# Loading the last two batches of an attention and Fourier-mixing kernel in natural token order

## The chip, the cores and the metric

The kernel runs on one core of a Trainium2 chip. A core has five engines, each with its own in-order stream of instructions: TensorE (PE in the profile; its weight loads are shown apart as PEld), VectorE (DVE), ScalarE (ACT), GpSimd (POOL) and SyncE (SP), which here only issues DMAs. DMAs are issued from the queues of SP, ACT and POOL, and all of them are carried out by the same 16 DMA engines. The metric is the device time in microseconds of one execution, the median of several runs.

## The reference

Four batches, 8 heads, 768 tokens, 64 numbers per head. First comes attention in which a token sees the first 8 keys (global) and the last 96 (local), with a bias that falls with distance; then, on the 768x512 result `x` of each batch, the real part of a two-dimensional Fourier transform, a normalization and a two-layer network with a ReLU:

```python
rel = pos[:, None] - pos[None, :]
is_global = pos[None, :] < 8
is_local = (rel >= 0) & (rel < 96)
dist = np.where(is_global & ~is_local, 96.0, np.abs(rel))
scores = scale * q @ k.T - slopes * dist          # -1e9 where neither holds
a = softmax(scores);  x = a @ v                   # heads side by side: (4, 768, 512)
X = np.fft.fft(np.fft.fft(x, axis=1), axis=2)
u = x + np.real(X)
un = (u - mean(u)) / np.sqrt(var(u) + 1e-6)
out = u + np.maximum(un @ w_ch1, 0.0) @ w_ch2     # 512 -> 2048 -> 512
```

## The kernel before

**Stages.** Each batch `b` goes through four stages. *Attention* works on pairs of heads (`hp` 0 to 3, numbered through as `n = 4*b + hp`): q and k are loaded and cast to fp16 (`load_qk`), transposed (`trans`), multiplied into three groups of scores (`score`, tile `sc`), passed through an exponential on ACT and multiplied by v (`av`, tile `pav`). The 8 global keys have their own small product (`glob`, tile `pgl`), for which the first 32 transposed keys were copied together into `kG` (`kg_copies`, line 494). *Mixing* folds the 768 tokens by their symmetries on VectorE (`fold_s`, `fold_d`), multiplies by a table of sines and cosines along the tokens (`y_unit`, line 933, tiles `py` and `zy`) and by a second one along the features (`u_unit`, line 1023, tile `pu`). Part of the results is also needed with its columns reversed: `mirror` (lines 968 to 970, tile `rev`) copies it on POOL. From batch 1 on the attention result also goes out to DRAM and back in another order (`bounce`, lines 735 to 745, `xd` and `xr`). *Normalization* (`centre`, lines 1108 to 1125, with a square root on POOL in the small tile `sm`) follows. The *network* runs in units `c = 3*b + pair`: eight `ph` units of 8 matmuls against the first weights (line 1178) and then `pg` units against the second (line 1211; from c = 8 on in a form with seven products for eight, `pgA` and `pgD`, line 1295). The sum of output and `u` (line 1220) is stored by SP (line 1225) or, for one pair of each batch, by an indirect DMA from POOL (line 1195).

**Token order.** Within each block of 128 tokens all four batches are kept with the even tokens in partitions 0 to 63 and the odd ones in partitions 64 to 127 (`tau` in the code). Batches 0 and 1 get this order from the way in which pairs of rows of 512 bytes are loaded and transposed on TensorE. Batches 2 and 3 (`b >= FB`) are loaded by half: for each pair of heads and each of q and k four loads (two halves of the partitions, two heads, line 433), and for v two loads (line 419), each taking every second row of 256 bytes. With eight loads for q and k and two for v that is 4 x 10 = 40 loads per batch, all issued from POOL's queue. Their transposes are DMA transposes on SP's queue (line 505). The masks, the distance matrix `dist_k` (copied on POOL at line 1447 from a tile `dist` that batches 0 and 1 use) and the transform's table `t1` follow the same order.

**The order of the work.** A planner in the kernel's own program (`Plan`) holds a modelled time for each engine, and takes at each step what can start first: a TensorE unit out of four streams (mixing, attention, `ph`, `pg`) or a waiting operation of another engine. Each operation has a price in us written beside it; `pl.later([("POOL", 1.0, fn)], needs, ...)` says engine, price, and what must be there. Where two engines are named, the one that ends sooner by the model gets it. A table `BIAS` shifts the start of single operations or groups of them, and so changes the order. Prices and table set only the order of the instructions in each engine's stream; on the chip each engine goes strictly through its own stream and waits on semaphores. A software DMA on POOL (`swq`) may have eight of its kind in flight in the model.

**Buffers.** q and k of n >= 6 rotate through 4 buffers, the transposed ones (`TT`) through 4, so batch 3's transposes wait for batch 2's scores and global products. The loads of batches 2 and 3 wait for the last weight load (`("wl", 7)`), those of v also for the end of the attention two batches before. There is one buffer for the mixing tiles `zy`, one for `rev`.

Of the kernel before, what the change touches and what calls it, by code (L numbers as in the profile page):

```python
# [14 lines left out]
P = 128  # L15
# [7 lines left out]
class Plan:  # L23
# [125 lines left out]
    def slot(self, tag):  # L149
# [7 lines left out]
    BIAS = {('h', 7, 2): 1.5, ('g0', '*', 1): 1.5, ('ss', '*', 7): 1.5, ('rd', '*', 10): -0.3, ('u', 3, 0): 1.5, (1, 19): 0.3,  # L157
# [88 lines left out]
def kernel(  # L246
# [23 lines left out]
    FB = 2  # L270
    DB = 0
# [12 lines left out]
    X3 = [(1, 1), (1, 2), (2, 1), (2, 2), (3, 1)]  # L284
# [7 lines left out]
    t1 = np.zeros((P, 4, 384))  # L292
    for r in range(4):
        th = 2.0 * np.pi * ((tau[:, None] * (6 * mm + r)) % S) / S
        t1[:, r, 0:128] = np.sin(th)
        t1[:, r, 128:256] = np.cos(th)
        t1[:, r, 256:384] = -np.sin(th)
    t1x = np.zeros((P, 5, 384))
    for n, (r, i) in enumerate(X3):
        th = 2.0 * np.pi * (((tau[:, None] + P * i) * (6 * mm + r)) % S) / S  # L300
        t1x[:, n, 0:128] = np.sin(th)
        t1x[:, n, 128:256] = np.cos(th)
        t1x[:, n, 256:384] = -np.sin(th)
# [21 lines left out]
    t1_d = nc.inline_tensor(t1.reshape(P, -1).astype(np.float16), name="t1m")  # L325
    t1x_d = nc.inline_tensor(t1x.reshape(P, -1).astype(np.float16), name="t1xm")
# [49 lines left out]
    t1_sb = kon.tile([P, 4, 384], FP16, tag="t1", name="t1")  # L376
# [38 lines left out]
    def load_v(b, hp):  # L415
        h0 = 2 * hp
        for t in range(2):
            def run(t=t):
                nc.gpsimd.dma_start(v16[b % 2][64 * t:64 * t + 64, h0:h0 + 2, :, 0:Dh].rearrange("m h i d -> m (h i) d"),  # L419
                                    v[b, h0:h0 + 2].rearrange("h (i m t) d -> t m (h i) d", m=64, t=2)[t])  # L420
            swq(run, 0.75, ([("avdone", b - 2), ("wl", 7)] if b > 1 else []), [("v", b, hp, t)], 0.7, b < 2)

    def load_qk(b, hp):
# [3 lines left out]
        for w, src in enumerate((q, k)):  # L427
            if b >= FB:
                for x in range(4):
                    def run(w=w, src=src, t=x // 2, h=x % 2):  # L430
                        if n not in qk16:
                            qk16[n] = buf(tag, ti, [P, 2, NS, 2, Dh], FP16, 1)
                        nc.gpsimd.dma_start(qk16[n][64 * t:64 * t + 64, w, :, h], src[b, h0 + h].rearrange("(i m t) d -> t m i d", m=64, t=2)[t])  # L433
                    swq(run, 0.65, free(tag, ti) + [("wl", 7)], [("qk", n, w, x)], 0.35, False)
# [1148 lines left out]
```

## Time and profile before

| | us |
|---|---|
| median of 3 runs | 262.11 |
| lowest, highest | 261.17, 262.74 |
| span of the profiled execution | 262.7 |
| TensorE busy | 246.2 (94%) |
| VectorE busy | 165.4 (63%) |
| ScalarE busy | 145.0 (55%) |
| GpSimd busy, DMA issue on it included | 116.0 (44%) |

The profiled execution's span, 262.7 us, is the time from its first to its last instruction; it stands 0.6 us above the median of the timed runs and beside the highest of them. In rows of the profile an engine's name comes first, then the line of the kernel (L433), the operation, the tiles as output<-input, and the number of instructions (x32); POOL's times for DMA_DIRECT2D are what issuing one load cost it. In lists of waits "A <- B: t, n, m" says that A stood t us in n waits, the longest m, until B had ended. In tables by stretch come, for each engine in the order PE, PEld, DVE, ACT, POOL, the busy us and the number of instructions, then TensorE's granted clock as a share of full speed, the DMA share (which counts packets in flight and can go over 1) and GB/s. In strips each digit is the busy tenths of one of 40 equal slices of 6.57 us.

### The profile page before, as it was taken

The page shows a single profiled execution, that of the slowest core. Times are in us where ns is not written, and L with a number is a line of the kernel's source. Part 1 is how long each engine was busy: PE and PEld are TensorE (multiplying, and loading weights), DVE is VectorE, ACT ScalarE, POOL GpSimd, SP SyncE. Part 2 cuts the span into 40 slices and gives each one's busy share as a digit, 9 for nine tenths or more (in the row PEclk, how much of TensorE's full clock was granted, in tenths as well). Part 3 has the DMA queues.
Part 4 walks back from the last instruction along what each step waited for, and adds up shares of the span by engine and source line. Part 5 has one row for each costly group of instructions (what it writes and reads, how often), then busy time and mean ns, then how long its engine had stood idle before and what let it go on. Part 6 is the DMA issues. An engine that isn't in the chain of part 4 may idle for free.

```text
span 262.7 us, 6833 instructions
## 1 busy us (share of the span) xinstructions
PE 246.2 (94%) x2838; PEld 177.1 (67%) x2838; DVE 165.4 (63%) x399; ACT 145.0 (55%) x243; POOL 116.0 (44%) x185
## 2 busy tenths in 40 slices
PE   7888989999999999997995899999999999999994
PEld 3557646689687664654572467579778668888883
DVE  4458995647884263541689348877996775634373
ACT  3579987785858645763325183694635445345300
POOL 9796664535889978999410303020201331010010
PEclk9999999999999999999999599999999999999999
DMA  7999999993999999999799501504063141401103
GB/s 193 164 162 181 275 206 120 160 182 26 184 197 193 132 145 151 124 103 151 146 102 200 172 2 80 137 26 44 2 160 120 51 101 52 120 2 40 40 22 140
DMA packets 93886, 31.56 MB, mean 120 GB/s; under 512 B 82368, under 2 KB 90560, under 8 KB 93856
## 3 DMA queue, kind: packets, MB, share of 16 engines
q0 software_dynamic: 66912, 17.06, 65.2%
q1 hardware_dynamic: 23616, 10.99, 21.1%
q10 hardware_dynamic: 3328, 3.08, 5.0%
q8 instruction: 22, 0.36, 0.6%
q14 instruction: 8, 0.07, 0.1%
HBM read 30.99 MB, written 8.65 MB: 151 GB/s over the span
## 4 chain that ended last, share of the span: by engine, by line
PE 51%; DMA 18%; POOL 18%; ACT 5%; issue 3%; SPq 1%; DVE 1%; POOLq 0%; ACTq 0%
PE ph L1178 18%; PE pg L1211 11%; POOL qk L433 10%; DMA qk<-in_k_dram 8%; PE pgD L1295 5%; DMA w<-in_moe_w_ch_dram 5%; PE pgA L1295 4%; POOL v L419 4%; DMA hT<-in_k_dram 3%; DMA qkT<-qk 3%; PE py L933 2%; ACT ex L605 2%; PE pav L695 2%; SPq L505 1%; PE pu L1023 1%
## 5 line engine op out<-in xcount | busy, mean ns | idle before, releaser
L1178 PE MATMUL ph<-unT,w 128*128 128x256 f16 x768 | 94.5, 275 | 0.0
L1178 PEld LDWEIGHTS <-w 128*128 128x128 f16 x768 | 73.6, 99 | 13.9 <-issue 2.6
L1184 ACT ACTIVATE hT<-ph 128x512 f16<-128x512 f32 x85 | 50.2, 597 | 54.5 <-PE ph L1178 54.1
L1211 PE MATMUL pg<-w,hT 128*128 128x512 f16 x256 | 61.4, 383 | 0.0
L1211 PEld LDWEIGHTS <-hT 128*128 128x128 f16 x256 | 24.4, 98 | 24.7 <-issue 1.7
L602 ACT ACTIVATE er<-sc 128x992 f16<-128x992 f32 (+2 forms) x24 | 21.7, 924 | 9.5 <-PE sc L577 6.3
L1124 POOL TENSOR_SCALAR sm<-sm 128x2 f32<-128x2 f32 x12 | 3.5, 293 | 52.0 <-ACT un L1117 51.7
L419 POOL DMA_DIRECT2D v<-in_v_dram x32 | 26.0, 863 | 0.9 <-DMA hT<-in_k_dram 0.6
L1220 DVE SCALAR_TENSOR_TENSOR u<-pg,sm,u 128x512 f32<-128x512 f32 x16 | 12.0, 750 | 19.3 <-PE pg L1211 12.9
L605 ACT ACTIVATE ex<-sc 128x992 f16<-128x992 f32 (+2 forms) x24 | 20.9, 928 | 5.8 <-PE sc L581 5.6
L433 POOL DMA_DIRECT2D qk<-in_q_dram x32 | 22.1, 778 | 3.3 <-DMA qk<-in_k_dram 2.3
L617 DVE TENSOR_TENSOR ex<-er,mk 128x992 f16<-128x992 f16 (+2 forms) x24 | 14.8, 629 | 13.4 <-ACT er L602 13.2
L433 POOL DMA_DIRECT2D qk<-in_k_dram x32 | 22.2, 825 | 0.9 <-DMA v<-in_v_dram 0.9
L1195 POOL DMA_INDIRECT out_dram<-u,back x4 | 4.6, 1142 | 39.3 <-DVE u L1313 21.0
L695 PE MATMUL pav<-v,ex 128*128 128x65 f16 x352 | 17.7, 193 | 0.0
L695 PEld LDWEIGHTS <-ex 128*128 128x128 f16 x352 | 16.0, 97 | 2.2 <-issue 1.0
L1117 ACT ACTIVATE un<-un 128x512 f16<-128x512 f16 x24 | 14.9, 621 | 4.3 <-PE ptu L1148 3.0
L1108 ACT ACTIVATE un<-u,sm 128x512 f16<-128x512 f32 x12 | 8.6, 721 | 12.1 <-DVE sm L1090 7.4
L688 PE MATMUL pav<-vG,eg 128*128 128x65 f16 x128 | 14.3, 193 | 0.9 <-DVE x L714 0.9
L948 ACT ACTIVATE zy<-py 128x1024 f16<-128x1024 f32 (+1 forms) x14 | 11.3, 841 | 6.1 <-PE py L933 5.6
L1295 PEld LDWEIGHTS <-hT 128*128 128x128 f16 x128 | 12.5, 98 | 1.8
L714 DVE TENSOR_TENSOR x<-pav,rc 128x384 f16<-128x384 f32 x24 | 12.6, 554 | 0.6
(147 smaller groups left out, 382.7 us busy)
## 6 DMA issues: line engine op xcount, KB each, us to landing
w<-in_moe_w_ch_dram POOLq DMA_DIRECT2D x8, 512.0 KB, 10.2
out_dram<-u SPq DMA_DIRECT2D x15, 256.0 KB
v<-in_v_dram POOLq DMA_DIRECT2D x32, 96.0 KB, 6.1
qk<-in_q_dram POOLq DMA_DIRECT2D x32, 48.0 KB, 4.7
qk<-in_k_dram POOLq DMA_DIRECT2D x32, 48.0 KB, 4.5
xr<-xd SPq DMA_DIRECT2D x3, 512.0 KB
xd<-x ACTq DMA_DIRECT2D x4, 384.0 KB
hT<-in_q_dram POOLq DMA_DIRECT2D x5, 192.0 KB, 7.2
```

Of the source, the lines that this page charges most:

```text
L419: nc.gpsimd.dma_start(v16[b % 2][64 * t:64 * t + 64, h0:h0 + 2, :, 0:Dh].rearrange("m h i d -> m (h i) d"), v[b, h0:h0 + 2].rearrange("h ( ...
L433: nc.gpsimd.dma_start(qk16[n][64 * t:64 * t + 64, w, :, h], src[b, h0 + h].rearrange("(i m t) d -> t m i d", m=64, t=2)[t])
L602: A(mine(), cut(pa), AF.Exp, 0.0, 0.125)
L605: A(cut(expst[hp][:, :, g * 512:g * 512 + (384 if g == 2 else 512)]), cut(pa), AF.Exp, 0.0, 0.125)
L617: VT(o, mine(), m, op=ALU.mult)
L688: nc.tensor.matmul(o[:, s * 65:(s + 1) * 65], EG[:, s, (j - 2) * P:(j - 1) * P], vG[b % len(vG)][:, hp, s, 0:65], start=True, stop=False, ...
L695: nc.tensor.matmul(o[:, s * 65:(s + 1) * 65], lhsT, v16[b % 2][:, 2 * hp + s, i, 0:65], start=(j < 2 and a == 0), stop=(a == len(ops) - 1) ...
L1117: A(x, x, AF.Square, accum_out=MV[c][:, a, 2:3])
L1178: nc.tensor.matmul(ph[:, a * CH:(a + 1) * CH].rearrange("p (x m) -> p x m", x=2), W1[0][:, d, jb * P:(jb + 1) * P], UNT[c][:, :, d, :], st ...
L1184: pl.later([("ACT", act(512), lambda: A(dst, ph, AF.Relu)), ("DVE", dve(512), lambda: V.tensor_scalar_max(dst, ph, 0.0))], [], e, [("h", c ...
L1211: nc.tensor.matmul(pg, HT[c][:, jb, t * P:(t + 1) * P], W2[0][:, jb, :], start=(jb == 0), stop=(jb == NJ - 1))
L1295: nc.tensor.matmul(o, lhs(j), rhs(j), start=(first and j == 0), stop=(j == NK - 1), skip_group_check=True)
```

## The change

Batches 2 and 3 are kept in natural token order: token m of a block in partition m.

- Loads: q and k of one head in one load of 128 partitions x 6 rows of 256 bytes, so 4 per pair of heads in place of 8; v of a pair of heads in one load in place of 2; 20 per batch in place of 40.
- The keys 0 to 31 now lie together in the transposed tile, so `glob` reads them there; the copies to `kG` are left out for these batches, and with them a wait (`gldone`).
- The distance matrix for these batches, `dist_k`, comes from a constant of its own by a DMA on SP after the last load of the first weights, in place of two copies on POOL.
- The table `t1` exists in both orders. The second one is loaded by SP into the buffer of the first, after the last `py` unit of batch 1.
- The attention result of a batch is written to DRAM by one DMA in place of two.
- The mirrored copies may run on GpSimd or VectorE (for all batches), whichever the planner picks.
- Prices: a q or k load 0.75 in place of 0.65 (on the DMA side 0.75 in place of 0.35), a v load 1.0 in place of 0.75 (1.5 in place of 0.7).
- The table `BIAS` is replaced by another, so the order of the instructions is new everywhere, for batches 0 and 1 too. Code that nothing used (`DB`, `X3`, `t1x`) is gone.

```diff
-    BIAS = {('h', 7, 2): 1.5, ('g0', '*', 1): 1.5, ('ss', '*', 7): 1.5, ('rd', '*', 10): -0.3, ('u', 3, 0): 1.5, (1, 19): 0.3,
...
+    BIAS = {('kG', 3): 3, (1, 2): 0.7, ('s', '*', 8): 0.3, ('mk1', '*', 2): 0.7, ('h', 1, 3): 0.3, ('v', 3, 2, 0): 6,
...
+    key = np.arange(P)[:, None]
+    rel = np.arange(2 * P)[None, :] - key
+    near = np.where((rel >= 0) & (rel < NL), rel, far)
+    distk = np.concatenate([np.where(near < far, rel, np.where(key < NG, NL, far)), near, near[:, 0:P]], 1)
...
+    t1 = np.zeros((2, P, 4, 384))
+    for x, tok in enumerate((tau, np.arange(P))):
...
     def load_v(b, hp):
         h0 = 2 * hp
+        if b >= FB:
+            def whole():
+                nc.gpsimd.dma_start(v16[b % 2][:, h0:h0 + 2, :, 0:Dh].rearrange("m h i d -> m (h i) d"),
+                                    v[b, h0:h0 + 2].rearrange("h (i m) d -> m (h i) d", m=P))
+            swq(whole, 1.0, [("avdone", b - 2), ("wl", 7)], [("v", b, hp, t) for t in range(2)], 1.5, False)
+            return
...
-                for x in range(4):
-                    def run(w=w, src=src, t=x // 2, h=x % 2):
+                for h in range(2):
+                    def run(w=w, src=src, h=h):
                         if n not in qk16:
                             qk16[n] = buf(tag, ti, [P, 2, NS, 2, Dh], FP16, 1)
-                        nc.gpsimd.dma_start(qk16[n][64 * t:64 * t + 64, w, :, h], src[b, h0 + h].rearrange("(i m t) d -> t m i d", m=64, t=2)[t])
-                    swq(run, 0.65, free(tag, ti) + [("wl", 7)], [("qk", n, w, x)], 0.35, False)
+                        nc.gpsimd.dma_start(qk16[n][:, w, :, h], src[b, h0 + h].rearrange("(i m) d -> m i d", m=P))
+                    swq(run, 0.75, free(tag, ti) + [("wl", 7)], [("qk", n, w, h)], 0.75, False)
...
         pl.later([("SP", 0.0, lambda: None)], [("xb", n, w) for w in range(2)], 0.0, [("qkT", n)], [("free", "qk", n - 6)])
-        kg_copies(b, hp)
...
-                    nc.tensor.matmul(pg[o:o + 32, s, :], kG[b % 2][r, n % HP, :],
+                    nc.tensor.matmul(pg[o:o + 32, s, :], kG[b][r, n % HP, :] if b < FB else TT[n][r, 1, 0:32],
...
+            if b >= FB:
+                eng.dma_start(XD[b].rearrange("(j m) d -> m j d", m=P), X[b])
+                return
...
-        pl.later([("POOL", 1.0, r0)], [("y", b, 0, 3), ("y", b, 3, 3)] + free("rev0", b), 0.0,
+        pl.later([("POOL", 1.0, lambda: r0(nc.gpsimd.tensor_copy)), ("DVE", 0.75, lambda: r0(V.tensor_copy))], [("y", b, 0, 3), ("y", b, 3, 3)] + free("rev0", b), 0.0,
...
+        swq(lambda: table(0, nc.gpsimd), 0.45, [], [("c", "t1", 0)], 1.2)
+        pl.later([("SP", 0.45, lambda: table(1, nc.sync))], [("t1u", 0)], 0.0, [("c", "t1", 1)], lat=1.6, dma=1.2)
+        dma_const(dist_k, distk_d, 0.5, ("dk",), [("w1", 3)])
...
-        for t in range(2):
-            r = slice(64 * t, 64 * t + 64)
-            pl.later([("POOL", 0.76, lambda r=r, t=t: nc.gpsimd.tensor_copy(dist_k[r, :], dist_sb[r, t, :]))],
-                     [("c", "dist")] + ([("us", 2, 1)]), 0.0, [("dk", t)], rank=3)
```

More of the change, by code (lines that the diff above doesn't have):

```diff
@@ L324 @@
     dist_d = nc.inline_tensor(dist.astype(np.float16), name="distm")
-    t1_d = nc.inline_tensor(t1.reshape(P, -1).astype(np.float16), name="t1m")
-    t1x_d = nc.inline_tensor(t1x.reshape(P, -1).astype(np.float16), name="t1xm")
+    distk_d = nc.inline_tensor(distk.astype(np.float16), name="distkm")
+    t1_d = [nc.inline_tensor(t1[x].reshape(P, -1).astype(np.float16), name=f"t1m{x}") for x in range(2)]
     t2_d = nc.inline_tensor(t2.reshape(P, -1).astype(np.float16), name="t2m")
@@ L375 @@
     gb_sb = kon.tile([P, 2], FP32, tag="gb", name="gb")
[L376 removed]
+    T1 = {}
     t2_sb = kon.tile([P, 4, 3, P], FP16, tag="t2", name="t2")
@@ L495, in cp @@
                            TT[n][:, 1, 0:P].rearrange("p (t m) -> p t m", t=2)[:, :, 0:16])
-        pl.later([("POOL", 0.25, lambda: cp(nc.gpsimd))] + [("DVE", 0.12, lambda: cp(V))] * (b == 0), [("qkT", n)] + ([("gldone", b - 2, hp % 2)] if b > 1 else []), 0.0,
+        pl.later([("POOL", 0.25, lambda: cp(nc.gpsimd)), ("DVE", 0.12, lambda: cp(V))], [("qkT", n)], 0.0,
                  [("kG", n)], [("free", "qkT", n)], rank=RA(b))
@@ L663, in run @@
             pl.later([("ACT", 2 * act(512), ex)], free("eg", b) + [("c", "gb")], e, [("eg", b, half) for half in halves], CD(b, ring), ring=ring, rank=RA(b))
-        ATT.append(([("kG", n) for n in ns], BANKS(b), run))
+        ATT.append(([("kG" if b < FB else "qkT", n) for n in ns], BANKS(b), run))
     X = {}
@@ L735, in wr @@
                 eng.dma_start(rows[t], X[b][64 * t:64 * t + 64])
-        pl.later([("ACT", 1.2, wr)], [("x", b, hp, z) for hp in range(HP) for z in range(2)], 0.0, [("xw", b)], [("free",) + XT[b]] * 2,
-                 lat=1.7, dma=3.0, nd=2)
+        pl.later([("ACT", 0.6 if b >= FB else 1.2, wr)], [("x", b, hp, z) for hp in range(HP) for z in range(2)], 0.0, [("xw", b)], [("free",) + XT[b]] * 2,
+                 lat=1.7, dma=3.0, nd=1 if b >= FB else 2)
         def rd():
@@ L935, in run @@
             e = pl.pe(mm_us(256, cnt), start)
-            if b < DB:
-                pl.used(("free", "hT", 3), e)
+            pl.used(("t1u", b // FB), e)
             if g == len(YG) - 1:
```

56 lines of the change are left out of this document (25 added, 31 removed), and 26 rows, old and new, of the table BIAS.

## The prediction

> **What bounds the kernel now.** I read the page first, for the shares and the strip of slices.
>
> ```profile
> span 262.7 us, 6833 instructions
> ...
> PE 246.2 (94%) x2838; PEld 177.1 (67%) x2838; DVE 165.4 (63%) x399; ACT 145.0 (55%) x243; POOL 116.0 (44%) x185
> ...
> PE   7888989999999999997995899999999999999994
> ...
> POOL 9796664535889978999410303020201331010010
> PEclk9999999999999999999999599999999999999999
> DMA  7999999993999999999799501504063141401103
> ```
>
> TensorE (PE) is the bound: 94% busy, and nothing else is above 67%. So only time in which PE stands still or runs at a low clock can be won. The digits show three such places: the start, slice 19 (a 7, from 118 us), and slices 22 and 23 (5 and 8, from 138 us, the clock 5 in slice 23). Busy time by stretch gives the sizes.
>
> ```profile
> 0.00:50.00 50.00, 43.41 (x813) 27.76 (x814) 34.26 (x121) 36.29 (x52) 35.92 (x57) 1.00 1.54 182
> 50.00:122.00 72.00, 72.00 (x746) 50.73 (x744) 39.40 (x85) 47.16 (x85) 57.39 (x87) 1.00 1.54 145
> 122.00:126.20 4.20, 1.77 (x27) 1.17 (x25) 0.42 (x1) 0.07 (x1) 3.72 (x11) 1.00 1.06 173
> ...
> 141.30:151.00 9.70, 5.78 (x28) 2.79 (x27) 5.49 (x11) 2.33 (x5) 2.58 (x4) 0.65 0.79 181
> 151.00:258.40 107.40, 107.40 (x1006) 84.48 (x1005) 72.00 (x154) 52.49 (x93) 13.71 (x22) 1.00 0.24 65
> ```
>
> The first figure after the length is PE. It is idle 6.59 us in the first 50, not at all in 50 to 122, 2.43 us in 122 to 126.2, 3.92 us in 141.3 to 151 (there at a clock of 0.65), and not at all from 151 to 258.4. The list of waits names the causes of the two holes in the middle.
>
> ```profile
> PE sc L577 <- DMA qkT<-qk: 3.9, 1, 3.9
> PE pu L1023 <- POOL rev L969: 1.8, 1, 1.8
> ...
> PE pgl L650 <- POOL kG L494: 0.6, 1, 0.6
> ```
>
> All three lead to GpSimd (POOL). Its timeline, and that of SP's queue:
>
> ```profile
> 62.89 0.84 POOL L419 DMA_DIRECT2D v<-in_v_dram  x1
> ...
> 120.28 2.00 POOL L419 DMA_DIRECT2D v<-in_v_dram  x2
> ...
> 123.64 0.21 POOL L968 COPY rev<-zy 128x2 f16<-128x2 f16 x1
> ...
> 125.71 0.36 POOL L494 COPY kG<-qkT 128x32 f16<-128x32 f16 x2
> 126.01 0.73 POOL L433 DMA_DIRECT2D qk<-in_q_dram  x1
> ...
> 127.12 16.38 SPq L505 DMA_TRANSPOSE qkT<-qk  x8
> ```
>
> From 62.89 to 126.74 POOL issues the 80 loads of batches 2 and 3 almost without a pause, 63.85 us. The mirrored copies of batch 1 come out at 123.64, behind the loads, though the products that they read were made by 79.8 (rows below); PE waits 1.81 us for them. The key copies come out at 125.7: 0.62 us. The third step is longer.
>
> ```profile
> DVE u L1220 <- POOL sm L1125: 6.4, 1, 6.4
> ```
>
> ```profile
> SPq L1225 <- DVE u L1220: 17.8, 3, 9.3
> ```
>
> (The second is SP's own list, from 100 to 147 us.) An addition on VectorE waited 6.4 us for POOL's small `sm` operation, which stands behind the same loads, and output stores on SP waited for such additions, 9.3 us in the longest wait. Batch 3's eight transposes stand behind those stores and start at 127.12, 16.38/8 = 2.05 us apart. One of them lands just before 145.25, where PE had stood for 3.92 us. What follows runs at half the clock:
>
> ```profile
> 126.12 0.40 PE L650 MATMUL pgl<-qkT,kG 64*32 64x512 f16 x6 [0.62 <-POOL kG L494]
> ...
> 145.25 0.59 PE L577 MATMUL sc<-qkT 64*128 64x256 f16 x4 [3.92 <-DMA qkT<-qk]
> ```
>
> ```profile
> 144.00:145.00 1.00, 0.00 (x0) 0.00 (x0) 0.97 (x3) 0.00 (x0) 0.00 (x0) 0.57 1.35 125
> 145.00:146.00 1.00, 0.75 (x5) 0.26 (x6) 0.96 (x2) 0.00 (x0) 0.73 (x2) 0.50 1.16 390
> ...
> 150.00:151.00 1.00, 1.00 (x7) 0.74 (x5) 0.00 (x0) 0.96 (x2) 0.00 (x0) 0.51 0.00 0
> 151.00:152.00 1.00, 1.00 (x11) 0.90 (x10) 0.47 (x1) 1.00 (x2) 0.00 (x0) 1.00 0.00 0
> ```
>
> From 145.25 to 151.0 PE runs at 0.50; 5.78 us of work there would have taken 2.9, so 2.9 us are lost. The 1.8 us hole was followed by no such stretch. The middle thus costs 2.43 + 3.92 + 2.9 = 9.2 us. That is the pot.
>
> **The loads.** Forty loads per batch become twenty, over all 128 partitions.
>
> ```profile
> L419 POOL DMA_DIRECT2D v<-in_v_dram x32 | 26.0, 863 | 0.9 <-DMA hT<-in_k_dram 0.6 <-DMA hT<-in_q_dram 0.3
> L433 POOL DMA_DIRECT2D qk<-in_k_dram x32 | 22.2, 825 | 0.9 <-DMA v<-in_v_dram 0.9
> L433 POOL DMA_DIRECT2D qk<-in_q_dram x32 | 22.1, 778 | 3.3 <-DMA qk<-in_k_dram 2.3 <-DMA qk<-in_q_dram 0.8
> L457 POOL DMA_DIRECT2D hT<-in_q_dram x5 | 4.4, 880 | 0.8 <-DMA hT<-in_q_dram 0.8
> ```
>
> By busy time a q or k load of 384 rows costs POOL (22.1 + 22.2)/64 = 0.69 us, a v load of 768 rows 26.0/32 = 0.81, a load of 768 longer rows at L457 0.88. Twice the rows cost far less than twice the time. New q and k loads have 768 rows: 0.86. New v loads have 1536, of which there is no row: at the least 0.81 (rows cost nothing), at the most two old ones, 1.63; along the line 0.69, 0.81 it is 1.05, which I take. Issue alone falls from 64 x 0.69 + 16 x 0.81 = 57 us to 32 x 0.86 + 8 x 1.05 = 36 us.
>
> But the data must also flow. At the start POOL issued 22 loads of 768 rows in a row:
>
> ```profile
> 1.35 1.04 POOL L457 DMA_DIRECT2D hT<-in_q_dram  x1
> ...
> 20.99 0.86 POOL L457 DMA_DIRECT2D qk<-in_k_dram  x1
> ```
>
> That is (21.85 - 1.35)/22 = 0.93 us for each 768 rows, waits for the DMA engines included. Batches 2 and 3 are 48 such units: 45 us, the lower end being the 36 of issue alone and the upper the 64 of before. Take 45, and 4 us of POOL's other work between: the last load goes out at about 112 in place of 126.7, 15 us earlier. The transposes of batch 3 can then start some 15 us earlier as well, and the one for which PE waited lands at about 130 in place of 145.2. PE needs it at 141.33 less the 2.43 of the earlier holes, 138.9. Some 9 us of cover: the hole and the slow clock go. If the loads took their 64 us again, the cover would be gone and the hole would end at 145.2 as before.
>
> [...]
>
> **Key copies.** Four POOL copies per batch go, and the global scores read the transposed keys in place: 0.62 us of PE, in the pot. The matmuls keep their shape. **Mirrored copies** may go to either engine: some 0.9 us on POOL (0.21, then two of some 0.4), and on VectorE I have no such row; between 0.2 and 0.9 by its small copies. VectorE is 63% busy, so either is nothing on the path; what matters is that they don't stand behind the loads: 1.81 us, in the pot.
>
> **The table of the first transform** is loaded a second time, into the same buffer, on SP, once batch 1 has used it.
>
> ```profile
> 79.42 0.38 PE L933 MATMUL py<-t,ww 128*128 128x256 f16 x2
> ...
> 154.29 1.04 PE L933 MATMUL py<-t,ww 128*128 128x256 f16 x8
> ...
> t<-t1m POOLq DMA_DIRECT2D x1, 384.0 KB, 8.4
> ```
>
> Last use by batch 1 at 79.8, first by batch 2 at 154.3: 74 us for a load that took 8.4. Even with batch 2 thirty us earlier it is hidden. SP waits for that last use, though, with transposes behind it: nothing if its place fits, bounded by the few us that PE runs behind the order.
>
> **The distance matrix** comes by DMA on SP in place of two POOL copies; the bounce of batch 2 and 3 is one DMA on ACT in place of two.
>
> ```profile
> 48.27 1.56 POOL L1447 COPY distk<-dist 64x640 f16<-64x640 f16 x2
> ...
> 137.08 1.29 ACTq L735 DMA_DIRECT2D xd<-x  x2
> ```
>
> 1.56 us at 48 us, where POOL then idles (its strip shows 3 and 5), and 0.65 us per batch on ACT, which is 55% busy: nothing on the path.
>
> **The new order** has no row. Its bounds: in the first 50 us the 6.59 us of idle PE can become a third less or more, 2 us either way, as the early loads are not touched; in the middle it can make a hole of its own. I charge one like the 1.81 us one, since the old order had one of this size even where its data was 40 us old.
>
> **Sum.** 262.7 (the profiled span) - 2.43 - 3.92 - 2.9 + 1.8 = 255.3. The median of the timed runs is 262.11, 0.6 under the span, so **254.7 us**.
>
> **Rivals.** *R1, the data set the pace.* The DMA strip is at 9 in slices 11 to 19, 66 to 125 us. If the engines and not POOL's issue made the 63.85 us, batch 3 comes when it came, the hole ends at 145.2 whatever was saved at 122, and the time is 262.1, no change. For it: the strip, and the waits of 2.3 and 0.8 us for landed loads. Against it: POOL's idle time before all such loads is 0.9 + 0.9 + 3.3 = 5 us, and the start moved 768 rows in 0.93 us against 2 x 0.69 here. *R2, part of it.* The order puts batch 3's scores earlier, and a hole of 2 to 4 us with a slow stretch of 2.9 stays: 262.1 - 9.2 + 3 + 2.9 = 258.8. For it: PE follows its order strictly, and attention of batch 3 moves forward with its data. *R3, slower.* The code prices a new q or k load at 0.75 us and v at 1.5 for the order; the start showed 0.93 per 768 rows. Over 48 units that is 48 x 0.18 = 8.6 us of drift by the end of batch 3. If batch 3's first scores stand where the prices say that data lands (62.9 + 36 = 99 us), PE stands those 8.6 us and then loses 2.9 to the clock; with the 1.8 charged above, 262.1 - 9.2 + 1.8 + 8.6 + 2.9 = 266.2. It decides from a hole of 5.8 us on (5.8 + 2.9 + 1.8 = 10.5, the pot and the 1.3 below). Against it: the old order drifted as much (64 x 0.65 + 16 x 0.75 = 53.6 priced, 63.85 taken) and the sum of its holes was 6.4; and batch 3 cannot begin before batch 2 has freed its buffers, and its global scores ran only at 126.12 here. *R4*, the edit does not do what it says: the 20 loads are in the code, so no chance is kept for it.
>
> **How the numbers follow.** Forecast 0.52, with 251 to 257.5 as its own range (2 us of start either way, one small hole more or less); R2 0.13; R1 0.10; R3 0.25, most of it over 263.5, since other misplacements of the new order would act in the same way. 0.5% is 1.3 us, about what a measurement can tell from no change. Faster 0.52 + 0.13 = 0.65, same 0.10, slower 0.25. The range: 250.5 (the whole pot, 252.9, and the start 2 better) to 263.5; about 0.16 is left above and 0.04 below.
>
> **What would show it.** Right: POOL's last load near 110, no PE wait for `rev` or `qkT`, no 5 in the clock strip after the start, transposes of batch 3 on SP before 120, stretch 50 to 150 with under 2 us of idle PE. The load step is wrong if 20 new loads take as long as 40 old ones; the table step if PE waits for `t` in a `py` matmul; the order step if the first 50 us have over 8.6 us of idle PE. The whole is wrong if a new hole of over 7 us stands in the middle.

## The result and the profile after

| | before | after |
|---|---|---|
| median, us | 262.08 | 256.77 |
| lowest, highest, us | 257.16, 265.62 | 255.82, 257.43 |
| runs | 20 | 20 |
| span of the profiled execution, us | 262.7 | 255.4 |

The changed kernel is faster: 5.3 us by the medians, with a ratio of the compared runs of 0.9893 [0.9866, 0.9921]. The ratio is formed from the quickest runs of each kernel (of before, those within 1.5% of its fastest), and so it is nearer to 1 than the medians' quotient of 0.980. What the table also shows is the spread: 8.5 us for before, 1.6 us for after.

The head of the page and the strips of the kernel after (each digit a slice of 6.39 us):

```profile
span 255.4 us, 6779 instructions
...
PE 244.0 (96%) x2838; PEld 176.2 (69%) x2838; DVE 172.0 (67%) x413; ACT 140.5 (55%) x237; POOL 89.0 (35%) x127
...
PE   7998687999999999999999999999999999999994
...
POOL 8788734208967428556001001110022104010010
PEclk9999999999999999999999999999999999999999
```

TensorE's strip has no hole after slice 7, and the clock strip no 5. GpSimd has 127 instructions for 185, and its strip has gaps in slices 12 to 19, where before's stood at 7 to 9. By stretch, with TensorE's busy time first, then PEld, DVE, ACT, POOL, the clock, the DMA share and GB/s:

```profile
0.00:50.00 50.00, 42.00 (x738) 26.16 (x742) 32.35 (x116) 36.16 (x52) 32.11 (x50) 1.00 1.61 193
50.00:122.00 72.00, 72.00 (x856) 51.84 (x848) 46.19 (x103) 45.22 (x85) 42.40 (x54) 1.00 1.51 152
122.00:150.00 28.00, 28.00 (x293) 17.62 (x293) 22.08 (x44) 13.76 (x19) 1.17 (x1) 1.00 0.89 143
150.00:250.00 100.00, 100.00 (x945) 78.98 (x944) 69.62 (x149) 45.33 (x82) 13.34 (x22) 1.00 0.25 69
```

From 50 to 250 us TensorE never stands. All of its idle time is in the first 50 us, 8.00 us where before had 6.59. The spans can be balanced with that: 9.2 us of holes and half clock are gone from the middle, 1.4 us is lost at the start, and TensorE's busy time apart from the clock is 0.7 us more (244.0 against 246.2 - 2.9): 9.2 - 1.4 - 0.7 = 7.1 of the 7.3 us between the two spans.

The list of TensorE's waits, after, has neither `qkT` of the DMA nor `rev` in it:

```profile
PE pz L1429 <- DVE eg L1424: 1.4, 1, 1.4
...
PE pgl L644 <- DVE kG L489: 0.5, 1, 0.5
```

The costs of a load came out as worked out: 0.86 us for 768 rows, 1.08 for 1536 (forecast 0.86 and 1.05). The groups of instructions by form:

```profile
L428 POOL DMA_DIRECT2D qk<-in_k_dram x16 | 13.6, 862 | 1.9 <-DMA v<-in_v_dram 1.7
L428 POOL DMA_DIRECT2D qk<-in_q_dram x16 | 13.6, 864 | 8.5 <-DMA qkT<-qk 4.8 <-DMA qk<-in_k_dram 3.6
...
L408 POOL DMA_DIRECT2D v<-in_v_dram x8 | 8.6, 1080 | 3.3 <-DMA qk<-in_k_dram 1.6 <-DMA v<-in_v_dram 1.6
```

Yet the loads as a whole took nearly as long. GpSimd's timeline, after (start, us, instruction, in brackets what it waited for):

```profile
60.10 1.76 POOL L428 DMA_DIRECT2D qk<-in_q_dram  x2
...
111.26 1.74 POOL L428 DMA_DIRECT2D qk<-in_q_dram  x2 [4.83 <-DMA qkT<-qk]
...
120.82 1.05 POOL L408 DMA_DIRECT2D v<-in_v_dram  x1
```

The 40 loads stretch from 60.10 to 121.87, 61.8 us, where the 80 took 63.85. GpSimd's busy time between the first and the last load fell from 58.8 to 40.7 us, but what was saved went into waits: in the list of its waits, 8.5 us ahead of loads for earlier loads in flight, 5.0 us for ScalarE's `un`, and 4.8 us, the longest, for a buffer that a transpose had not read yet.

What changed around the hole at `qkT` shows in the places of batch 2's and batch 3's scores. TensorE's timeline, before and then after:

```profile
86.31 0.39 PE L577 MATMUL sc<-qkT 64*128 64x256 f16 x4
...
138.63 0.59 PE L577 MATMUL sc<-qkT 64*128 64x256 f16 x8
```

```profile
105.84 0.39 PE L571 MATMUL sc<-qkT 64*128 64x256 f16 x4
...
120.69 0.41 PE L644 MATMUL pgl<-qkT 64*32 64x512 f16 x8
...
134.72 0.59 PE L571 MATMUL sc<-qkT 64*128 64x256 f16 x8
```

Before, batch 2's scores began at 86.31 and its last global scores came at 126.12, 40 us later. After, they begin 20 us later, at 105.84, and the global scores stand at 120.69. With them the transposed tiles come free, and SP's queue, after, goes on at once (its timeline, the same in a shorter window, and its list of waits from 100 to 150 us):

```profile
105.56 26.05 SPq L500 DMA_TRANSPOSE qkT<-qk  x10
...
121.12 4.08 SPq L500 DMA_TRANSPOSE qkT<-qk  x3
```

```profile
SPq L500 <- PE ph L1171: 12.2, 2, 11.6
```

Three of these ten belong to batch 2 and seven to batch 3. The seven start at 121.12, right as the global scores end (120.69 + 0.41), and no store stands between. That is 6.0 us earlier than before's 127.12, and they stand 1.50 us apart ((105.56 + 26.05 - 121.12)/7), before's 2.05. The list puts the wait of 11.6 us to the network unit next in TensorE's stream, which starts at 121.04; that the global scores end it rests on the code, where they are the last to read these tiles, and on `old_st` below, whose list names them.

### The profile page after: what moved, and what is told of

It is laid out like the page before. It is cut to its first block, busy times and chain, and to the rows that moved or that the text cites. A ratio compares the mean times of both kernels' runs of the same rounds, so it can differ in the third digit from the quotient of the medians.

```text
span 255.4 us, 6779 instructions
## 1 busy us (share of the span) xinstructions
PE 244.0 (96%) x2838; PEld 176.2 (69%) x2838; DVE 172.0 (67%) x413; ACT 140.5 (55%) x237; POOL 89.0 (35%) x127
## 3 DMA queue, kind: packets, MB, share of 16 engines
q0 software_dynamic: 66272, 17.06, 67.1%
## 4 chain that ended last, share of the span: by engine, by line
PE 89%; DVE 7%; ACT 2%; issue 1%; ACTq 0%
PE ph L1171 33%; PE pg L1204 22%; PE pgD L1288 6%; PE pgA L1288 4%; PE pav L687 4%; PE py L927 3%; PE pu L1016 3%; PE pz L1429 3%; PE sc L571 3%; PE pt L521 2%; ACT ex L599 2%; PE pav L680 1%; PE sc L549 1%; PE pu L991 1%; DVE qkT L528 1%; DVE x L706 1%
## 5 line engine op out<-in xcount | busy, mean ns | idle before, releaser
L1171 PE MATMUL ph<-unT,w 128*128 128x256 f16 x768 | 92.5, 273 | 0.0
L1177 ACT ACTIVATE hT<-ph 128x512 f16<-128x512 f32 x77 | 45.7, 598 | 46.9 <-PE ph L1171 46.5
L1204 PE MATMUL pg<-w,hT 128*128 128x512 f16 x256 | 60.4, 379 | 0.0
L1178 DVE TENSOR_SCALAR hT<-ph 128x512 f16<-128x512 f32 x19 | 13.0, 688 | 7.8 <-PE ph L1171 7.7
L428 POOL DMA_DIRECT2D qk<-in_q_dram x16 | 13.6, 864 | 8.5 <-DMA qkT<-qk 4.8
L740 POOL DMA_INDIRECT xr<-xd,back x3 | 4.0, 1338 | 35.6 <-DVE ex L611 17.2
L1101 ACT ACTIVATE un<-u,sm 128x512 f16<-128x512 f32 x11 | 7.8, 720 | 14.4 <-DVE sm L1083 10.0
L414 POOL DMA_DIRECT2D v<-in_v_dram x16 | 12.1, 766 | 7.2 <-DMA w<-in_moe_w_ch_dram 5.6
L428 POOL DMA_DIRECT2D qk<-in_k_dram x16 | 13.6, 862 | 1.9 <-DMA v<-in_v_dram 1.7
L941 ACT ACTIVATE zy<-py 128x1024 f16<-128x1024 f32 (+1 forms) x13 | 10.3, 827 | 6.8 <-PE py L927 6.5
```

Of the source, the lines that this page charges most:

```text
L428: nc.gpsimd.dma_start(qk16[n][:, w, :, h], src[b, h0 + h].rearrange("(i m) d -> m i d", m=P))
L1171: nc.tensor.matmul(ph[:, a * CH:(a + 1) * CH].rearrange("p (x m) -> p x m", x=2), W1[0][:, d, jb * P:(jb + 1) * P], UNT[c][:, :, d, :], st ...
L1177: pl.later([("ACT", act(512), lambda: A(dst, ph, AF.Relu)), ("DVE", dve(512), lambda: V.tensor_scalar_max(dst, ph, 0.0))], [], e, [("h", c ...
L1178: ("DVE", dve(512), lambda: V.tensor_scalar_max(dst, ph, 0.0))],
L1204: nc.tensor.matmul(pg, HT[c][:, jb, t * P:(t + 1) * P], W2[0][:, jb, :], start=(jb == 0), stop=(jb == NJ - 1))
```

## The experiments

Theory A, that of the prediction: the merged loads do it, since they bring batch 3's data sooner. Theory B: the new order does it, by where it puts batch 2's scores, and the loads, copies and tables of the change are worth little by themselves. All times are medians; each run's kernel before ran on the same chip beside it.

**The unchanged pair again**, to see the spread and a second profile of each.

> The kernel before once more, with a second profile. If the first profile was a typical one, its holes in the middle are again 6.4 us and the slow stretch again 2.9, and span plus what lies around it is within 0.5 us of its median. If the first profile showed more than the usual holes, as its span plus the 1.8 us that lie around the span of the changed kernel (264.5) would say, the holes are smaller now by 2 us or more and the span is near 260.

> The changed kernel once more, beside the kernel before and the next three on one chip. Both theories: no hole between 50 and 250 us, time 256 to 257.5 with a spread of under 2 us between its runs. If splitting its loads was worth something, it stands 1 us or more under the 258.2 of the split version; if not, it reads 258 here too.

Before: 260.98 us (258.99 to 263.32, 12 runs). After: 256.87 (256.15 to 257.6, 6 runs), ratio 0.9837 [0.9786, 0.9887], no holes again. The second profile of before has a span of 258.4 at a time of 260.15, and other holes. TensorE's timeline, and the stretches with the clock (the figure before the last two):

```profile
125.17 0.28 PE L1023 MATMUL pu<-t,rev 128*128 128x128 f16 x2 [3.24 <-POOL rev L969]
127.07 0.57 PE L650 MATMUL pgl<-qkT,kG 64*32 64x512 f16 x6 [0.62 <-POOL kG L494]
```

```profile
127.00:128.00 1.00, 0.93 (x8) 0.26 (x9) 1.00 (x4) 0.28 (x1) 0.87 (x3) 0.59 0.00 0
128.00:129.00 1.00, 1.00 (x4) 0.44 (x3) 0.93 (x6) 1.00 (x3) 0.70 (x1) 0.50 0.70 100
...
130.00:131.00 1.00, 1.00 (x11) 0.49 (x10) 0.00 (x0) 0.13 (x1) 0.00 (x0) 0.71 0.86 143
```

Its timeline of SP:

```profile
128.06 13.55 SPq L505 DMA_TRANSPOSE qkT<-qk  x8
```

Here the mirror's hole is 3.24 us with a slow stretch behind it, and the `qkT` hole is missing, though batch 3's transposes start 0.9 us later than in the first profile: they stand 13.55/8 = 1.69 us apart in place of 2.05, and TensorE, held up before, reaches batch 3's scores only at 141.06 in place of 138.63. So neither the start of the transposes nor an early hole decides by itself what is lost. The holes of the prediction are real and stand where it put them, but their sizes change from one execution to the next. And in each of the 20 runs of after the time was 1.72 to 1.83 us above the span: a span is no time. By this offset the first profile of before, 262.7, was an execution of some 264.4 (an estimate), 2.4 over the median of 262.08. Some of that lay at the start: TensorE was idle there for 5.89 us in the second profile, for 6.59 in the first.

**The loads alone, in both orders.** `merged_old` is before with whole loads (it leaves out the even-odd order, so batches 2 and 3 are computed with their tokens permuted):

```diff
+                if b >= FB:
+                    if t == 0:
+                        nc.gpsimd.dma_start(v16[b % 2][:, h0:h0 + 2, :, 0:Dh]..., v[b, h0:h0 + 2]...)
+                    return
...
-                        nc.gpsimd.dma_start(qk16[n][64 * t:64 * t + 64, w, :, h], src[b, h0 + h]...[t])
+                        if t == 0:
+                            nc.gpsimd.dma_start(qk16[n][:, w, :, h], src[b, h0 + h].rearrange("(i m) d -> m i d", m=P))
```

`split_new` is after, with each of the 40 loads issued as two halves of 64 partitions, at the same place of the order:

```diff
-                nc.gpsimd.dma_start(v16[b % 2][:, h0:h0 + 2, :, 0:Dh]..., v[b, h0:h0 + 2]...)
+                for t in range(2):
+                    r = slice(64 * t, 64 * t + 64)
+                    nc.gpsimd.dma_start(v16[b % 2][r, h0:h0 + 2, :, 0:Dh]..., v[b, h0:h0 + 2]...[r])
```

> Kernel of before, every engine's order as it was, but each load of batches 2 and 3 for the first half of the partitions is now one load of all 128 partitions in natural order and the second one is left out (so these two batches are computed with their tokens permuted: the even-odd order is left out). L, the loads: POOL's last load goes out near 112 us in place of 126.7, the waits of TensorE for rev and kG (2.4 us) and for qkT (3.9 us, 2.9 us of slow clock) go; span near 254, time 255 to 257. O, the order: the rows arrive at the same pace as before (last landing within 5 us of before, the engines set it), the hole at qkT stays, time within 2 us of before's median.

> Kernel of after, every engine's order as it is there, but each of the 40 loads of batches 2 and 3 is issued as two loads of 64 partitions (80 loads again, natural order kept). L: POOL is again full of loads until about 126 us, TensorE gets holes of 4 us or more between 100 and 150 us, time 260 or more. O: no holes, time within 1 us of after's 256.8, since the rows come at the pace of the DMA engines and the new order does not use them earlier.

`merged_old`: 263.87 us (258.04 to 270.44, 6 runs) beside 261.0. Five of the six stand at 263.1 or above and one at 258.04, so no gain is shown, and a small one is not excluded; the profiled execution is one of 269.02. Its timelines, of GpSimd, SP and TensorE:

```profile
113.82 1.16 POOL L421 DMA_DIRECT2D v<-in_v_dram  x1
```

```profile
115.76 15.74 SPq L1231 DMA_DIRECT2D out_dram<-u  x3
131.67 16.45 SPq L511 DMA_TRANSPOSE qkT<-qk  x8
```

```profile
101.44 0.59 PE L583 MATMUL sc<-qkT 64*128 64x256 f16 x4 [2.16 <-DMA qkT<-qk]
```

The last load went out at 113.82 + 1.16 = 115.0, 11.8 us before that of before and 3 from the 112 forecast. Batch 3's transposes nevertheless started at 131.67, 4.5 us later than the 127.12 of before, behind three stores. In this execution theory A fails: the data was there (by the medians these loads landed 6.0 to 6.6 us after their issue, so near 122), and the queue that uses it was not free. `split_new`: 258.17 (255.99 to 262.47, 12 runs), ratio 0.989 [0.9853, 0.9927], with one hole at TensorE:

```profile
117.15 0.59 PE L575 MATMUL sc<-qkT 64*128 64x256 f16 x8 [1.49 <-DMA qkT<-qk]
```

In the new order the merger is worth 258.17 - 256.87 = 1.3 us (on two chips), about the price of this hole.

**The order alone.** `BIAS` is emptied in after (`flat_new`) and in before (`flat_old`), so that the planner orders by its prices only:

```diff
-    BIAS = {('kG', 3): 3, (1, 2): 0.7, ('s', '*', 8): 0.3, ('mk1', '*', 2): 0.7, ('h', 1, 3): 0.3, ('v', 3, 2, 0): 6,
...
+    BIAS = {}
```

> Kernel of after with an empty table of shifts (order by the model alone). O: several us slower than after, 259 to 266, as the table is what removes holes. L: within 2 us of after, holes in the middle under 2 us, and 5 us or more under flat_old.

> Kernel of before with an empty table of shifts. O: 262 to 270, and within 2 us of flat_new. L: 5 us or more above flat_new, with TensorE waiting for rev, kG or qkT behind POOL's loads.

`flat_new`: 263.1 us (261.88 to 264.17, 12 runs), ratio 1.009 [1.0058, 1.0122]. `flat_old`: 261.61 (260.8 to 264.29, 12 runs), ratio 1.0062 [1.0026, 1.0099]. With both tables empty the change's parts give nothing, or 1.5 us the wrong way. From `flat_new` to `after_again` it is 6.2 us, and only the table differs. What stands still in `flat_new` is a chain of another kind, TensorE's timeline and the stretch around it:

```profile
103.03 0.45 PE L1131 MATMUL ptu<-ident,un 64*64 64x64 f16 x32 [2.39 <-DVE u L1070]
105.25 0.65 PE L1131 MATMUL ptu<-ident,un 64*64 64x64 f16 x32 [1.77 <-DVE unT L1143]
```

```profile
103.00:116.00 13.00, 11.19 (x137) 8.04 (x137) 6.90 (x17) 8.30 (x17) 8.07 (x12) 0.74 2.01 195
```

The sum `u` of batch 1 came late (VectorE itself waited 2.8 us for the bounced `xr`), and the clock of 0.74 over 13 us shows the slow stretch behind.

**Batch 2's scores 15 us sooner** in after's table, which undoes the feature of the new order that stands out (`new_sooner`):

```diff
+    for _k in range(51, 63):
+        BIAS[(1, _k)] = BIAS.get((1, _k), 0.0) - 15.0
```

> Kernel of after with the scores of batch 2 moved earlier in TensorE's order by a shift of 15 us in the table (40 loads as in after): they start after 43 units of network work in place of 50, batch 3's after 59 in place of 73. If it is the place of the attention in TensorE's order that gives cover, waits for qkT come back, 3 us or more with a slow stretch, and the time is 260 or more. If the loads gave the cover, no hole, and within 1 us of after.

268.5 us (267.78 to 269.73, 6 runs), ratio 1.0294 [1.0236, 1.0352]. By stretch:

```profile
50.00:122.00 72.00, 65.34 (x772) 44.47 (x765) 42.58 (x98) 44.88 (x80) 41.66 (x52) 0.95 1.63 160
```

6.66 us of idle TensorE come back in the stretch where after has none, and a clock of 0.95 over 72 us. But neither expectation had the cause. TensorE's list of waits and SP's timeline:

```profile
PE sc L574 <- ACT er L599: 3.0, 2, 2.1
...
PE sc L574 <- DMA qkT<-qk: 0.6, 1, 0.6
```

```profile
114.40 15.77 SPq L503 DMA_TRANSPOSE qkT<-qk  x8
```

With batch 2's scores sooner, batch 3's transposes do start sooner, at 114.40, 12.7 us ahead of before's; there is hardly a wait for `qkT`, and the kernel is the slowest of all. The scores, now packed closer, wait for ScalarE's exponentials (`er`) instead. So late scores keep that stretch full, but here not by covering the transposes, and an early start of the transposes brings nothing by itself.

**Copies moved alone, in the old order.** `old_dve` runs the mirrored copies of batch 1 and the key copies of batch 2 on VectorE:

```diff
-            nc.gpsimd.tensor_copy(rev[:, 1], src[:, 1, :, ::-1])
+            on = V if b == 1 else nc.gpsimd
+            on.tensor_copy(rev[:, 1], src[:, 1, :, ::-1])
...
-        pl.later([("POOL", 0.25, lambda: cp(nc.gpsimd))] ...
+        pl.later([("POOL", 0.25, lambda: cp(V if b == 2 else nc.gpsimd))] ...
```

> Kernel of before, order as it was, but batch 1's mirrored copies and batch 2's key copies run on VectorE at the place in the program that they had on POOL. If the holes add up, as the sum of the prediction has it, the waits for rev and kG (2.4 us) go and the time falls by 2.4 to 258.6. If the last hole hides the earlier ones, the wait for qkT grows by as much and the time stays within 1 us of before's 261.

261.89 us (259.7 to 267.35, 12 runs), no difference (ratio 1.0003 [0.9968, 1.0039]). TensorE's timeline in an execution of 263.53:

```profile
125.90 0.40 PE L650 MATMUL pgl<-qkT,kG 64*32 64x512 f16 x6 [1.77 <-DVE kG L494]
145.38 0.39 PE L577 MATMUL sc<-qkT 64*128 64x256 f16 x4 [4.43 <-DMA qkT<-qk]
```

The mirror's hole is gone, but the wait for the key copies is 1.77 us in place of 0.62, and the scores that wait for batch 3's transposes start at 145.38, as in before at 145.25. The holes do not add up: what is won at an early one is stood off at the later ones.

**The copies, in the new order.** `new_rev_pool` puts the mirrored copies of batches 0 and 1 back on GpSimd, `new_kg` the key copies of batches 2 and 3; `new_split_rev` is `split_new` and `new_rev_pool` together, `new_undo` all three.

```diff
-        ... ("DVE", 0.75, lambda: r0(V.tensor_copy))], ...
+        ... ("DVE", 0.75, lambda: r0(nc.gpsimd.tensor_copy if b < 2 else V.tensor_copy))], ...
```

```diff
+        def kc():
+            nc.gpsimd.tensor_copy(kG[b % 2][:, hp, :], TT[n][:, 1, 0:32])
+        pl.later([("SP", 0.0, kc)], ...
...
-                    nc.tensor.matmul(pg[o:o + 32, s, :], kG[b][r, n % HP, :] if b < FB else TT[n][r, 1, 0:32],
+                    nc.tensor.matmul(pg[o:o + 32, s, :], kG[b % 2][r, n % HP, :],
```

> Kernel of after, same order, but the mirrored copies of batches 0 and 1, which the planner gave to VectorE, run on POOL at the same place in the program. If freeing them from POOL's loads is worth what the prediction took (1.8 us), TensorE waits 1 to 3 us for rev near 82 us and the time is 258 to 259.5. If not: no wait over 0.5 us, within 0.7 us of 256.9.

> Kernel of after, same order, merged loads, mirrored copies where the planner put them, with only the key copies of batches 2 and 3 back on POOL. If they cost what the prediction took (0.62 us) or less: 256.5 to 258. If they hold up POOL's loads behind their wait for the transposes: a wait for qkT, 259 or more.

> Kernel of after, same order on the other engines, with the three physical parts undone together: loads split in two (80 again), the mirrored copies of batches 0 and 1 on POOL, and the global keys of batches 2 and 3 copied to kG on POOL, one copy when a pair of heads is transposed. O, the order: 258 to 260, still 1.5 us or more under before's 261.2. L, the parts: at or over before, 261 or more, with waits for rev, kG and qkT.

> Kernel of after, same order, with split loads and the mirrored copies of batches 0 and 1 on POOL. If these two stand in for each other, the wait for rev is 8 to 9 us again with a slow stretch, near 267. If the key copies were needed for it, under 2 us of wait and 258 to 260.

| kernel | median, us (lowest to highest) | ratio |
|---|---|---|
| `new_rev_pool` | 256.91 (255.81 to 257.97) | 0.9855 [0.98, 0.991] |
| `new_kg` | 256.7 (255.85 to 257.22) | 0.9837 [0.9802, 0.9872] |
| `new_undo` | 267.21 (265.63 to 268.21) | 1.0241 [1.0182, 1.03] |
| `new_split_rev` | 266.9 (265.92 to 268.17) | 1.0234 [1.0195, 1.0274] |

(Six runs each; the ratio is to before.) One by one, mirror and key copies are worth nothing and the merger 1.3 us. Mirror and merger together are worth 10: `new_split_rev`'s timelines of TensorE and GpSimd show why. `new_undo` also answers theory B: the new order, held as it is, with the old loads and copies is 2.4% slower than before.

```profile
91.27 0.40 PE L1020 MATMUL pu<-t,rev 128*128 128x128 f16 x2 [8.70 <-POOL rev L966]
```

```profile
87.56 3.12 POOL L410 DMA_DIRECT2D v<-in_v_dram  x4
90.51 0.38 POOL L965 COPY rev<-zy 128x2 f16<-128x2 f16 x1
```

With twice the loads ahead of it in GpSimd's stream the copy comes 8.7 us too late. Fewer loads (`new_rev_pool`), or another engine for the copy (`split_new`), each remove that by themselves: neither list of TensorE's waits has `rev` in it. The two edits insure each other, and neither shows a worth when only it is undone.

**A mixed order.** To keep the first 50 us of the planner without a table and the rest of after, the table is ignored until the modelled time is 50 us (`hyb50`) or 60 (`hyb60`):

```diff
-        if name is None:
+        if name is None or self.t["PE"] < 50:
```

> Kernel of after with the table of shifts ignored until TensorE's modelled time is 50 us. With an empty table the first 50 us had 5.8 us of idle TensorE, with the new one 8.0; batch 2's and 3's scores stand where they stand in after (50 to 99 units of network work). If the idle of the start and the cover in the middle are separate things: 254.5 to 255.5, faster than both. If the order after 50 us depends on the start: a hole in the middle, 257 to 262.

> The same with the table ignored until 60 us: as the last, with batch 3's scores 3 units of network work earlier; 254.5 to 255.5 if the start alone decides, a hole at qkT of batch 3 and over 257 if those 3 units (2.6 us) were the cover.

264.06 us (261.39 to 265.5, 12 runs) and 264.61 (264.19 to 266.24, 6 runs). By stretch, `hyb50`:

```profile
0.00:50.00 50.00, 44.04 (x794) 27.73 (x794) 35.09 (x129) 34.98 (x50) 33.07 (x52) 1.00 1.62 194
50.00:122.00 72.00, 67.07 (x740) 46.70 (x725) 43.72 (x94) 38.70 (x72) 41.76 (x52) 1.00 1.49 151
```

Two of the 8.00 us are won at the start, and 4.93 us stood still behind it; the longest waits are for VectorE's `unT` and `u` (2.0 and 1.2 us) as in `flat_new`, and none is for `qkT`. `hyb60`'s two longest are the same two (1.6 and 2.1 us), so the hole at `qkT` that its expectation named is not there either. The start of after can't be mended by itself in this way.

**What holds batch 3's transposes.** `old_all` is before's order with all three parts (merged loads, mirror of batch 1 on VectorE, keys in place; the even-odd order left out as in `merged_old`). `old_st` adds to it that GpSimd issues the three stores that stand ahead of batch 3's transposes on SP:

```diff
-                nc.sync.dma_start(out[b].rearrange("(m r) d -> m r d", r=6)[:, rs, :], UT[c][:, t, :])
+                on = nc.gpsimd if (c, t) in ((2, 0), (2, 1), (3, 0)) else nc.sync
+                on.dma_start(out[b].rearrange("(m r) d -> m r d", r=6)[:, rs, :], UT[c][:, t, :])
```

> Kernel of before, every other engine's order as it was, with merged loads, batch 2's and 3's global keys read in place and batch 1's mirrored copies on VectorE (the even-odd order of the tokens of batches 2 and 3 is left out). If the parts bring the gain and the new order only keeps it: no waits for rev or kG, under 2 us for qkT, 256 to 258. If the order is needed: waits for qkT of 3 us or more with a slow stretch, 260 or more.

> Kernel old_all (all three parts in the old order; the even-odd order of the tokens of batches 2 and 3 left out) with the three output stores that stand ahead of batch 3's transposes on SP's queue issued by POOL. If the stores hold the transposes: they start at 113 to 117 us, when the last loads land, the wait for qkT goes and the time falls to 259 to 261. If the place of batch 2's global scores in TensorE's order holds them: the first transpose still starts within 2 us after those scores (near 127), the wait for qkT stays 3 us or more, 263 to 266.

`old_all`: 265.4 us (261.48 to 266.27, 6 runs), ratio 1.0119 [1.0047, 1.0191]. SP's and TensorE's timelines:

```profile
112.98 15.24 SPq L1234 DMA_DIRECT2D out_dram<-u  x3
128.39 16.22 SPq L513 DMA_TRANSPOSE qkT<-qk  x8
```

```profile
146.71 0.59 PE L585 MATMUL sc<-qkT 64*128 64x256 f16 x4 [4.56 <-DMA qkT<-qk]
```

The loads and copies of the change without its order, and the kernel is slower than before: its last load is out at 114.6, the transposes start at 128.39, and the hole is there. `old_st`: 259.18 (258.19 to 262.49, 5 runs), ratio 0.9948 [0.9886, 1.0011]. Its list of SP's waits, its SP timeline (whole, then in a shorter window) and its list of TensorE's waits:

```profile
SPq L513 <- PE pgl L658: 24.2, 1, 24.2
```

```profile
97.88 42.37 SPq L513 DMA_TRANSPOSE qkT<-qk  x9
...
126.42 2.63 SPq L513 DMA_TRANSPOSE qkT<-qk  x2
```

```profile
PE sc L585 <- DMA qkT<-qk: 1.1, 2, 0.8
```

With the stores out of the way the transposes stand 24.2 us for batch 2's global scores and start at 126.42, 2.0 us sooner. In the profiled execution, of 258.35, the hole falls from 4.56 to 1.1 and its slow stretch goes; two of the five runs, 261.75 and 262.49 at a mean clock of 0.987, still have one. Each expectation is right by half: the global scores hold the start, and the stores the time. By the medians it is 6.2 us of time (on two chips) for 2.0 us of start, more than the start can give; the transposes also follow each other faster, (97.88 + 42.37 - 126.42)/8 = 1.73 us apart in place of 16.22/8 = 2.03. So there are two conditions for the start, the tile buffers, which only batch 2's scores on TensorE free, and SP's queue; and the pace behind it counts as well.

## Why the prediction was right and where it failed

- **Bound and place of the loss: right.** TensorE's holes and the clock behind them were the pot, and with them gone the span is 255.4, against the 255.3 of the sum. That the two agree so closely is partly luck: the 1.8 us charged for a hole of the new order is not there, and 1.4 us at the start and 0.7 us of busier TensorE, neither of them charged, stand in its place.
- **The baseline: mis-sized.** "The median of the timed runs is 262.11, 0.6 under the span" set a span against times. A time stood about 1.75 us above its span (1.72 to 1.83 in the 20 runs of after, 1.73 to 1.82 in the 12 of `before_again`), so the profiled execution was one of some 264.4, with holes above the usual. A median run had some 2.4 us less to lose, of which up to 0.7 at the start, so by this estimate its pot was nearer 7 than 9.2, and by their times that of the quickest runs of before was smaller still. So a forecast gain of 7.4 us (262.11 - 254.7) became 5.3 by the medians, and 1.1% by the ratio of the compared runs. Set rightly, the sum gives 255.3 + 1.75 = 257.05, beside 256.77 measured; the 2.1 us between the forecast of 254.7 and the result are this term. (In the range, the whole pot and a start 2 better make 250.9, not 250.5.)
- **"The transposes of batch 3 can then start some 15 us earlier as well": the step that failed.** They start 6.0 us earlier in after, and in the old order with the merged loads not earlier at all (128.39 and 131.67). They wait for batch 2's global scores (24.2 us in `old_st`) and for SP's queue, whose stores ended last in before, `merged_old` and `old_all`. Before's global scores were at 126.12, in a row that the prediction quoted; of its own rival R3 it even said that batch 3 cannot begin before batch 2 has freed its buffers, and did not apply that to its own forecast. No gain from earlier loads alone is shown (`merged_old`, `old_all`), and where the transposes did start 12.7 us earlier (`new_sooner`), the kernel was slower.
- **"The last load goes out at about 112": right for the old order** (114.6 and 115.0), wrong for after (121.87), where GpSimd waits for a buffer (4.8 us) and for landings (8.5 us). Against `split_new`, whose last load is issued at 131.2, the merger still brings it 9.4 us forward. The old order with the same bytes (17.06 MB on the software DMA queue in both) went 12 us faster through its loads (52.0 in `old_all` against 63.85), and before's GpSimd was busy for 58.8 of 63.8 us there, so its issue had been part of the pace.
- **Mirrored and key copies (1.81 and 0.62 us, "in the pot"): right as holes, wrong as terms.** `old_dve` shows that they don't add to the last hole, and the new order doesn't need either edit alone. On VectorE the two large mirrored copies took 0.22 us each, on GpSimd 0.39.
- **Second table, distance matrix, one write of the bounce, at nothing: right.** No `py` matmul waits for `t`, and none of the three appears in the list of TensorE's waits.
- **The order: the wrong sign.** It was charged 1.8 us for a hole of its own. It has none after 50 us, loses 1.4 us at the start (2.1 against the second profile of before; 2 were allowed), and with the parts in place it is worth 6.2 us (`flat_new` to after). It does not carry the gain alone: with the old loads and copies it takes 267.21 us (`new_undo`), as the parts without it take 265.4 (`old_all`). The gain is that of the two together, which the prediction's sum, term by term, could not show.
- **The rivals.** R1's mechanism was half true, since the new loads took 61.8 us for the old 63.85; its time of 262.1 was not, since in the new order TensorE has no wait for `qkT` left. R3's drift of prices did not show in after. Slower versions exist all around it (`flat_new`, `old_all`, `new_sooner`), each by the holes of an order that does not fit, as R3 has it, but only `old_all`'s is mainly a wait for `qkT`.

**What stays open.** The number of transposed-tile buffers was not changed, so whether a fifth would free batch 3 from batch 2's scores was not tried. What sets the pace of the transposes, 1.50 us apart in after, 1.69 and 2.05 in the two profiles of before, was not tried either, though in the old order the hole at `qkT` goes with it: 3.9 us or more at 2.03 to 2.06 us apart, 1.1 or none at 1.69 and 1.73. Why before's holes change from run to run is not settled: they stand at the ends of DMA and GpSimd chains, and that chance in the transfers moves them is only argued. No version tried beat after; `new_kg` and `new_rev_pool` equal it.

## What to carry to other kernels

Before earlier data is counted as a gain, ask of the step that uses it what else it waits for: the buffer that it writes, and the queue that it is issued from; whichever ends last sets the start (here the buffers in `old_st`, after a wait of 24.2 us, and the queue in `old_all`, whose stores held it until 128.2 us). Test an edit's parts under one order and an order under one set of parts, and undo parts in pairs, since two edits that remove the same wait each look worth little alone (256.91 us with one undone, 258.17 with the other, 266.9 with both). And compare a profiled execution with the timed runs by its time, not its span (1.72 to 1.83 us less in after), most of all where the holes vary from run to run.

## What the runs showed of the hardware

In these runs a slow stretch came after short holes too. In before, 1.81 and 0.62 us of waits in a row left the clock at 1.00 in every microsecond from 122 to 132; 3.24 and 0.62 at the same place, in its second profile, were followed by half clock (0.59 and then 0.50 from 127 us). In `merged_old` it followed on waits of 0.73, 1.02 and 2.16 us within 6 us, and in `flat_new` the clock halved in the second of its two holes (2.39 and 1.77 us; 0.99 from 103 to 104 us, 0.50 in the next), with 0.45 us of matmuls between them. By stretch, `merged_old` and then `flat_new`:

```profile
100.00:101.00 1.00, 0.00 (x0) 0.00 (x0) 0.00 (x0) 0.00 (x0) 0.00 (x0) 0.76 1.95 125
...
107.00:108.00 1.00, 1.00 (x5) 0.45 (x4) 0.00 (x0) 0.00 (x0) 1.00 (x4) 0.83 3.26 136
```

```profile
104.00:105.00 1.00, 0.00 (x0) 0.12 (x1) 1.00 (x3) 1.00 (x4) 1.00 (x2) 0.50 2.43 155
```

Every microsecond between these two of `merged_old` shows 0.50. So a mean of 0.76 is read as half clock from 100.5 on, one of 0.83 as half clock until 107.3: 6.8 us, of which 5.9 were work (from 101.44). Read in the same way, the work at half clock was 5.7 us in before, 5.9 in `new_split_rev` and 4.5 in `old_all`, but 3.4 in `old_dve` and in the second profile of before. So a hole cost, in these runs, its length, where no later wait took it up, and where the clock dropped half of that work more, some 1.7 to 3 us (an estimate from the 3.4 to 5.9 us of work at a clock of 0.50). How much idle time makes the clock drop, and how much work brings it back, no run shows by itself.
